# A top-k attention kernel with a gated feed-forward block: where the sine, the gate and the argument reduction stand in the first twelve units

## The chip, the cores and the metric

The kernel runs on one core of one Trainium2 chip. Its time is the device time in microseconds (us) of one execution; lower is better. A core has five engines with a queue of instructions each: TensorE (PE, with its weight loads PEld), VectorE (DVE), ScalarE (ACT), GpSimd (POOL) and SyncE (SP), which here only issues DMAs. Each queue is worked off in order, and engines wait for one another by semaphores.

## What is computed

The reference takes q, k and v of 8 batches, 8 heads, 576 positions and a head size of 64, and keeps in each row of scores the 32 largest:

```python
scores = scale * np.matmul(q, k.transpose(0, 1, 3, 2))
kth = np.partition(scores, -top_k, axis=-1)[..., -top_k:-top_k + 1]
scores = np.where(scores >= kth, scores, -1000000000.0)
scores = scores - np.max(scores, axis=-1, keepdims=True)
attn = np.exp(scores)
attn = attn / (np.sum(attn, axis=-1, keepdims=True) + 1e-09)
...
h = x @ w_in
g = h * np.cos(h)
return (g @ w_out).astype(np.float32)
```

Here x is the attention's output with the heads side by side: 4608 rows of 512. The weights w_in (512 x 2048) and w_out (2048 x 512) arrive as 64-bit numbers and are turned into 32-bit ones on the chip.

## The kernel before

The work is cut into 144 units. A unit is 128 rows of queries of one pair of heads; four units with the same rows make a block, whose feed-forward part can start when all four are done. The loop at the end runs over the units, and its body `slot(i, u, w, x, z)` is one slot of a software pipeline written out by hand: VectorE searches the top 32 of unit u = i, ScalarE masks and exponentiates unit w = i - 1, GpSimd splits unit x = i - 2 into 16-bit halves (L424, L426) which SyncE writes out and reads back transposed (L434, L440), and in even slots TensorE multiplies units z = i - 4 and i - 3 with v (`values`, L477). Scores of coming units (`scores`, L226) are computed in even slots, mostly for two units at once; `take_scores` (L236, L237) copies them out of PSUM on ScalarE.

Between these stand steps of the feed-forward part, handed to TensorE by `feed(n)` as a credit allows: `ff1` (L537, xT by w_in into mm) and `ff2` (L612, g by w_out into o). For each 1024 columns of a block there is a chain: `take_first` copies mm/(2 pi) into g (L551) and a rounded value into x (L553) on ScalarE; the argument is reduced on GpSimd in two steps, `reduce_first` (L573) and `reduce_second` (L582); `sines` computes the cosine as a sine on ScalarE (L592, another table than the exponential's); `gate` multiplies g by it on GpSimd (L599). A block has two such chains. `feed` lets `ff2` begin some feeds after the gate was recorded (`can_second`), and only for weights that were added in an earlier slot.

The dictionary `ff` carries a flag `late`. When it is set, `take_first` marks its result with the slot's number and `reduce_first` leaves a result of the same slot for the next one. Before the change it is off in a slot's first half and on in the second.

In the first slots the weights are decoded as well: `load_weights` at a slot's start (L120, on SyncE's queue in slots 0 and 1, then on ScalarE's), `decode_first` on ScalarE (L133, L136) near its end, and in the following slot `decode_second` on VectorE (a shift, L144) and `decode_third` on GpSimd (an integer add, L154). The last add, of w_out15, stands in slot 12.

In units 7 to 11 (`BUSY`) VectorE makes both folds of the scores (L247, L255); in the others that fold, GpSimd makes the lower one (L265, L274).

Of the kernel before, what the change touches and what calls it, by code (L numbers as in the profile page):

```python
# [30 lines left out]
def kernel(  # L31
# [16 lines left out]
    NP = H // 2  # L48
# [47 lines left out]
    ff = {"live": 0, "tick": 0, "now": 0, "credit": 0.0, "end": False, "kind": 0, "half": 0, "open": 0, "late": False}  # L96
# [6 lines left out]
    def load_weights(n, queue):  # L103
        for _ in range(n):
            i = wq["next"]
            if i >= len(chunks):
                return
            src, dst = chunks[i]
            if not DECODE:
                queue.dma_start(out=dst, in_=src)  # L110
                wq["next"] = wq["done"] = i + 1
                continue
            spare = i < 3 * XB and i % 2 == 1 and staged(1) < XB
            if spare:
                st = ffw.tile([P, CW, 2], I32, tag="x", name="st", bufs=XB)
            elif staged() + ff["live"] >= CHUNKS:
                return
            else:
                st = ffw.tile([P, CW, 2], I32, tag="g", name="st", bufs=CHUNKS)
            queue.dma_start(out=st.rearrange("p w i -> p (w i)"), in_=src)  # L120
            wq["loaded"].append((st, dst, int(spare)))
            wq["next"] = i + 1
# [16 lines left out]
    def decode_second(n):  # L139

        for _ in range(min(n, len(wq["second"]))):
            st, w, spare = wq["second"].popleft()
            wi = w.bitcast(I32)
            nc.vector.tensor_scalar(  # L144
                out=wi, in0=wi, scalar1=3, scalar2=None, op0=ALU.logical_shift_left
            )
            wq["third"].append((st, w, spare))
# [144 lines left out]
    def topk_first(u, w):  # L292

        u["top"] = tops[u["n"] % len(tops)]
        merges = w and w["folds"]
        if merges:
            merge_first(w)
        if u["folds"]:
            if u["n"] not in BUSY:
                fold_sum(u)  # L300
            fold_high(u)
        else:
            u["rest"] = work.tile([P, 2, S], F32, tag="rest", name="rest", bufs=1)
        if merges:
            merge_second(w)
        if u["folds"] and u["n"] in BUSY:
            fold_now(u)
        topk_round(u, 0, [lambda: bounds(w), lambda: distances(w)] if w else ())

    def topk_round(u, rnd, between=(), ahead=None):  # L310
        top, rest, lasts = u["top"], u["rest"], TOPK // 8 - 1
        end = TOPK - 1 - 8 * rnd
        at = top[:, :, end : end - 8 if rnd < lasts else None : -1, 0]
        if u["folds"]:
            search(
                at, rest[:, :, HS:S] if rnd == 0 else rest[:, :, 0:HS], rest[:, :, 0:HS], rnd < lasts,
                between if rnd < lasts else (),
            )
        else:
            search(at, u["s"] if rnd == 0 else rest, rest, rnd < lasts, between)  # L320
        if rnd < lasts:
            return
        del u["rest"]
        if u["folds"]:
            low = u.pop("low")
            for k in range(TOPK // 16):
                more = k < TOPK // 16 - 1
                if ahead and not more:
                    take_values(ahead)
                search(  # L330
                    top[:, :, 1 + 8 * k : 9 + 8 * k, 1], low, low, more,
                    () if more or rnd < lasts else between,
                )
# [16 lines left out]
    def search(to, src, rest, more, between=()):  # L350
        for j in range(2):
            nc.vector.max(to[:, j], src[:, j])  # L352
            if between:
                between[j]()
        if more:
            for j in range(2):
                nc.vector.match_replace(rest[:, j], to[:, j], src[:, j], NEG)  # L357
# [61 lines left out]
    def split(u):  # L419


        s = u.pop("s").rearrange("p j k -> p (j k)").bitcast(U16)
        halves = work.tile([P, 2, 2 * S + P], U16, tag="halves", name="halves", bufs=1)
        nc.gpsimd.tensor_copy(out=halves[:, :, 0 : 2 * S], in_=s.rearrange("p (k h) -> p h k", h=2))  # L424
        rden = u.pop("rden").bitcast(U16).rearrange("p (j h) -> p h j", h=2)
        nc.gpsimd.tensor_copy(  # L426
            out=halves[:, :, 2 * S :].rearrange("p h (j d) -> p h j d", j=2),
            in_=rden.unsqueeze(3).to_broadcast([P, 2, 2, D]),
        )
        u["halves"] = halves  # L430

    def write_halves(u):
        rows = u["rows"] = dram.tile([P, 2, 2 * S + P], U16, tag="rows", name="rows")
        nc.sync.dma_start(out=rows, in_=u.pop("halves"))  # L434

    def transposes(u):
        rows = u.pop("rows").rearrange("q h k -> (q h) k")
        pT = u["pT"] = work.tile([P, 2 * NT + 2, P], F32, tag="pT", name="pT", bufs=3)
        words = pT.rearrange("p c q -> p (c q)").bitcast(U16)
        nc.sync.dma_start_transpose(  # L440
            out=words.rearrange("p (c q) -> p c q", c=2 * NT + 2), in_=rows
        )
# [36 lines left out]
    def take_values(us):  # L479
        blk, hp, n = block_of[us[0]["tok"]], us[0]["hp"], len(us)  # L480
        if "xT" not in blk:
            blk["xT"] = work.tile([P, NP, P], F32, tag="xT", name="xT", bufs=5)
        for i, u in enumerate(us):
            to, o, pT = blk["xT"][:, hp + i], room[0][:, i * P : (i + 1) * P], u.pop("pT")
            if u["paired"]:
                nc.vector.tensor_tensor(out=to, in0=o, in1=pT[:, 2 * NT + 1], op=ALU.mult)
            else:
                nc.scalar.copy(out=to, in_=o)
        blk["left"] -= n
        blk["tick"] = ff["tick"]  # L490
# [94 lines left out]
    def sines(least):  # L585

        n = sum(c[3] < ff["now"] for c in waiting)
        if n == 0 or (n < least and waiting[0][3] + 2 > ff["now"]):
            return
        for _ in range(n):  # L590
            blk, g, x, _ = waiting.popleft()
            nc.scalar.activation(out=x, in_=x, func=AF.Sin, bias=halfpi, scale=TWO_PI_BELOW)  # L592
            sined.append((blk, g, x))

    def gate(n):
        for _ in range(min(n, len(sined))):
            blk, g, x = sined.popleft()
            eng = nc.vector if ff["end"] else nc.gpsimd
            eng.tensor_tensor(out=g, in0=g, in1=x, op=ALU.mult)  # L599
            blk["gated"].append(ff["tick"])  # L600
# [87 lines left out]
    for n in range(NP, len(order)):  # L688
        i = last[order[n - 5]] if n >= 5 else 0
        load_at(max(i, 2 * NP + 2), load_qk, *order[n])  # L690
        i = last_values[order[n - 6]] if n >= 6 else 0
# [13 lines left out]
    def send(x):  # L705

        split(x)
        write_halves(x)
        transposes(x)

    def slot(i, u, w, x, z):
        n = (3, 4, 3, 2)[i] if i < NP else 2 if i < 2 * NP else 3
        if i < NP:
            for load, b, hp in at_once[i]:
                load(b, hp)
        load_weights(n, nc.sync if i < 2 else nc.scalar)
        if x:
            send(x)
        ff["late"] = False
        topk_first(u, w)  # L720
        fold_low(u)
        topk_round(u, 1)
        topk_round(u, 2)
        decode_second(NP)
        decode_third()
        reduce_first()
        reduce_second()
        made = scored.get(i, [])
        if z:
            take_banks()  # L730
        feed(1)

        for m in made:
            scores(m)
        if z:
            values(z)


        late = len(made) > 0

        decoding = i < 3 * NP
        if i % 2 or decoding:
            sines(1)
        if w:
            mask(w)
        take_banks()
        if w and late:
            exponentials(w)
        take_scores(units[i + 1])
        if w and not late:  # L750
            exponentials(w)
        topk_round(u, 3, both(w), z)
        ff["late"] = True
        if i in at_slot:
            load, b, hp = at_slot[i]
            load(b, hp)
        gate(1)
        feed(1 if len(made) == 2 else 2)
        take_banks()
        decode_first(NP)  # L760
        reduce_first()
        reduce_second()
        feed(1 if len(made) == 2 else 3)
        if i == LAST:
            sines(1)
# [110 lines left out]
```

## Time and profile before

| what | value |
|---|---|
| median of 8 runs | 1468.9 us (1467.34 to 1471.08) |
| the profiled execution | 1469.89 us |
| its span, first to last instruction | 1468.1 us |
| mean granted clock of TensorE | 0.985 |
| busy: PE, PEld | 1390.7 us (95%), 998.2 us (68%) |
| busy: DVE, ACT, POOL | 1362.2 us (93%), 1087.9 us (74%), 1156.7 us (79%) |
| largest shares of the chain that ended last | PE 84%, DVE 8%, ACT 4%, DMA 2% |
| one shift of weights on VectorE (L144) | 0.419 us median |
| one table load on ScalarE | 1.28 us |

A line of the timeline gives the start and the length in us, the engine, the line of the kernel, the operation, the tile written and those read, how many instructions are merged, and in brackets how long the engine sat idle before and for whom. A line of waits gives the engine and line that waited, for whom, the total in us, how often, and the longest. A line of a table by stretch gives the stretch, its length, the busy time and instructions of PE, PEld, DVE, ACT and POOL, then TensorE's granted clock, the busy share of the DMA engines and GB/s. One matmul of 32-bit numbers leaves two records in the trace, so a step of `ff2` (two matmuls) is four records of L612, and a step of `ff1` (eight matmuls) sixteen of L537.

### The profile page before, as it was taken

To read this page: it belongs to the slowest core of one execution; us is meant where nothing else is said; L and a number is where in the kernel's file an instruction comes from. 1 tells how busy PE (TensorE), PEld (TensorE's weight loads), DVE (VectorE), ACT (ScalarE), POOL (GpSimd) and SP (SyncE) were. 2 spreads that over 40 slices of the span, in tenths; PEclk is the share of its full clock that TensorE was granted. 3 is DMA by queue.
4 is the path that set the end of the run, shared out by engine and by line. 5 is a ranking of instruction groups with operands and counts; after the bars stand their busy time and mean duration, and the time that the engine had idled before them with its cause. 6 is when DMAs were issued, how large, how long until landed. Compare 5 with 4: busy or idle time off the path is not lost.

```text
span 1468.1 us, 30229 instructions
## 1 busy us (share of the span) xinstructions
PE 1390.7 (95%) x10288; PEld 998.2 (68%) x10288; DVE 1362.2 (93%) x5213; ACT 1087.9 (74%) x1910; POOL 1156.7 (79%) x812
## 2 busy tenths in 40 slices
PE   4367999999999999999999999999999999999998
PEld 2254767777777767777777767777777777777765
DVE  7997999999999999999999999999999999999831
ACT  5786777777777777777777777777777777777651
POOL 5856888888888887888888888888888888888410
PEclk9788999999999999999999999999999999999999
DMA  8986586656665566657655666657665565655200
GB/s 259 276 232 172 161 196 176 159 162 174 189 159 151 153 185 180 167 145 192 181 167 146 149 179 181 173 151 183 188 168 146 151 171 168 162 151 151 62 8 15
DMA packets 427434, 240.00 MB, mean 163 GB/s; under 512 B 375952, under 2 KB 392592, under 8 KB 427280
## 3 DMA queue, kind: packets, MB, share of 16 engines
q1 hardware_dynamic: 418704, 216.88, 56.1%
q10 hardware_dynamic: 8576, 21.19, 4.2%
q8 instruction: 81, 1.33, 0.4%
q14 instruction: 73, 0.60, 0.1%
HBM read 45.09 MB, written 101.19 MB: 100 GB/s over the span
## 4 chain that ended last, share of the span: by engine, by line
PE 84%; DVE 8%; ACT 4%; DMA 2%; SPq 0%; issue 0%; POOL 0%; ACTq 0%; POOLq 0%
PE o L612 32%; PE mm L537 32%; PE rim L477 10%; PE sc L226 8%; DVE top L352 3%; DVE rest L357 2%; PE rim L226 2%; DMA v<-in_v_dram 1%; ACT s L391 1%; DMA st<-in_moe_w_in_dram 1%; DVE rest L247 1%; ACT s L383 1%; DMA pT<-rows 0%; ACT L391 0%; DVE low L357 0%
## 5 line engine op out<-in xcount | busy, mean ns | idle before, releaser
L537 PEld LDWEIGHTS mm<-xT,w_in 128*128 128x128 f32 x4608 | 539.4, 193 | 70.0 <-issue 64.3
L612 PE MATMUL o<-w_out,g 128*128 128x512 f32 x1152 | 539.1, 602 | 22.7 <-POOL g L599 19.4
L537 PE MATMUL mm<-xT,w_in 128*128 128x128 f32 x4608 | 542.4, 276 | 3.2 <-ACT x L553 2.5
L352 DVE MAX8 top<-rest 128x8 f32<-128x288 f32 x1148 | 481.0, 454 | 0.0
L424 POOL COPY halves<-s 128x2304 uint16<-128x2304 uint16 x140 | 294.5, 2104 | 150.3 <-ACT s L391 149.7
L357 DVE MATCH_REPLACE8 rest<-top,rest 128x288 f32<-128x288 f32 (+1 forms) x860 | 377.2, 446 | 0.0
L612 PEld LDWEIGHTS o<-w_out,g 128*128 128x128 f32 x1152 | 203.4, 191 | 211.7 <-issue 187.4
L352 DVE MAX8 top<-low 128x8 f32<-128x288 f32 x568 | 240.3, 449 | 0.0
L391 ACT ACTIVATE s<-s,nd 128x576 f32<-128x576 f32 x288 | 220.2, 767 | 0.8
L383 ACT ACTIVATE s<-s,top 128x576 f32<-128x576 f32 x288 | 206.1, 765 | 0.0
L274 POOL TENSOR_TENSOR low<-low,rest 128x576 int32<-128x576 int32 x137 | 193.4, 1412 | 10.7
L265 POOL TENSOR_TENSOR low<-s 128x576 int32<-128x576 int32 x137 | 193.2, 1410 | 6.3 <-ACT s L237 5.1
L226 PE MATMUL sc<-k,q 64*128 64x448 f32 (+1 forms) x640 | 158.8, 590 | 34.2 <-DVE rest L247 13.5
L551 ACT ACTIVATE g<-mm 128x512 f32<-128x512 f32 x144 | 85.8, 596 | 129.6 <-PE mm L537 125.5
L582 POOL TENSOR_TENSOR x<-g,x 128x1024 f32<-128x1024 f32 x68 | 160.8, 2365 | 5.7
L477 PE MATMUL rim<-pT,v 128*64 128x128 f32 (+1 forms) x2560 | 158.7, 268 | 3.3 <-DMA pT<-rows 3.3
L599 POOL TENSOR_TENSOR g<-g,x 128x1024 f32<-128x1024 f32 x68 | 160.7, 2363 | 1.3 <-ACT x L592 1.3
L477 PEld LDWEIGHTS rim<-pT,v 128*64 128x64 f32 x2560 | 132.0, 138 | 13.8 <-issue 5.0
L236 ACT COPY s<-sc 128x896 f32<-128x896 f32 x144 | 129.2, 897 | 12.0 <-PE sc L226 11.6
L237 ACT COPY s<-rim 128x256 f32<-128x256 f32 x144 | 55.0, 382 | 94.5 <-PE rim L477 94.5
L357 DVE MATCH_REPLACE8 low<-top,low 128x288 f32<-128x288 f32 x284 | 123.8, 444 | 0.0
L226 PEld LDWEIGHTS sc<-k,q 64*128 64x128 f32 (+1 forms) x640 | 47.3, 182 | 98.3 <-DVE rest L357 47.9
(59 smaller groups left out, 1333.5 us busy)
## 6 DMA issues: line engine op xcount, KB each, us to landing
rows<-halves SPq DMA_DIRECT2D x140, 640.0 KB, 3.0
out_dram<-ob ACTq DMA_DIRECT2D x36, 256.0 KB, 2.2
q<-in_q_dram SPq DMA_DIRECT2D x31, 288.0 KB, 3.7
v<-in_v_dram SPq DMA_DIRECT2D x32, 256.0 KB, 3.5
st<-in_moe_w_out_dram ACTq DMA_DIRECT2D x16, 512.0 KB, 5.0
st<-in_moe_w_in_dram SPq DMA_DIRECT2D x10, 512.0 KB, 6.7
k<-in_k_dram SPq DMA_DIRECT2D x31, 144.0 KB, 3.6
k<-in_k_dram SPq DMA_DIRECT2D x32, 128.0 KB, 3.7
```

Source lines behind the costliest of these rows:

```text
L226: nc.tensor.matmul(to[r0 : r0 + rows, j, 0 : k1 - k0], st["q"][d, q0 : q0 + rows], st["k"][d, k0:k1], start=True, stop=True,)
L265: nc.gpsimd.tensor_tensor(out=u["low"].bitcast(I32), in0=s[:, :, 0:HS], in1=s[:, :, HS:S], op=ALU.add)
L274: nc.gpsimd.tensor_tensor(out=low, in0=low, in1=u["rest"][:, :, HS:S].bitcast(I32), op=ALU.subtract)
L352: nc.vector.max(to[:, j], src[:, j])
L357: nc.vector.match_replace(rest[:, j], to[:, j], src[:, j], NEG)
L383: nc.scalar.activation(out=s[:, j], in_=s[:, j], func=AF.Prelu, bias=less[:, j, 1:2], scale=1.0, alpha=FAR)
L391: nc.scalar.activation(out=s[:, j], in_=s[:, j], func=AF.Exp, bias=nd[:, j : j + 1], scale=SCALE, accum_out=den[:, j, 0:1],)
L424: nc.gpsimd.tensor_copy(out=halves[:, :, 0 : 2 * S], in_=s.rearrange("p (k h) -> p h k", h=2))
L477: nc.tensor.matmul(o[d, to], lhsT, rhs, start=c == 0, stop=c == NT)
L537: nc.tensor.matmul(mm[:, at : at + w], w_in[f // FC][:, c, (f % FC) * P : (f % FC + 1) * P], blk["xT"][:, c], start=c == 0, stop=c == NC - 1,)
L582: nc.gpsimd.tensor_tensor(out=x, in0=g, in1=x, op=ALU.subtract)
L612: nc.tensor.matmul(o, g[:, at : at + P], w_out[f], start=f == 0, stop=f == NF - 1)
```

## The change

`decoding` is true in slots 0 to 11 and is now set at the slot's start. In these slots `sines(1)` and `gate(1)` are called after the third round of the search and so ahead of the weights' shifts and adds; the split of `send(x)` already stands before them. The call of `sines` in the middle of the slot is left to odd slots from 12 on. The gate of the slot's second half (L757 before) stays for all slots; in a decoding slot it finds something only if the first call left it. The flag `late` stays off in the second half of a decoding slot, so that a result of `take_first` is reduced at the end of the same slot.

```diff
         if x:
             send(x)
+        decoding = i < 3 * NP
         ff["late"] = False
         topk_first(u, w)
         fold_low(u)
         topk_round(u, 1)
         topk_round(u, 2)
+        if decoding:
+            sines(1)
+            gate(1)
         decode_second(NP)
         decode_third()
         reduce_first()
@@
-        decoding = i < 3 * NP
-        if i % 2 or decoding:
+        if i % 2 and not decoding:
             sines(1)
         if w:
             mask(w)
@@
         topk_round(u, 3, both(w), z)
-        ff["late"] = True
+        ff["late"] = not decoding
```

By the two programs' instruction order, VectorE's queue is unchanged, and PE's differs only from the last `ff1` step of the first block to that of the second. On GpSimd the first reduction moves from behind slot 8's adds to before slot 8's split, the first gate from slot 9 to slot 8 (behind the split, ahead of the adds of w_out6 and w_out5), and the second gate ahead of slot 10's adds instead of behind them. On ScalarE the first sine moves from slot 9's middle to slot 8's start, and the second stays the first activation of slot 10; in slot 12 the copies of mm (L551, L553) come before the sine instead of after the mask.

## The prediction

> **What bounds the kernel now.** I read the busy tenths of the page first, then stages, then who waited, then the queues around the longest wait. I call a slot by the number i of its unit; on VectorE the slots begin at 79.8 (slot 7), 90.1, 100.8, 111.6 (slot 10), 134.1, 144.7, 154.5 and 165.2 us (slot 14), read from the group of L340, which opens a slot. The busy time by slot:
>
> ```profile
> 100.80:111.60 10.80, 0.00 (x0) 0.00 (x0) 10.69 (x40) 10.74 (x19) 8.10 (x7) 0.60 0.56 187
> 111.60:134.10 22.50, 15.90 (x85) 8.92 (x86) 12.90 (x43) 11.12 (x19) 15.77 (x10) 0.74 0.63 176
> 134.10:144.70 10.60, 9.39 (x62) 7.29 (x60) 10.60 (x40) 9.51 (x19) 3.40 (x4) 1.00 0.79 187
> ...
> 165.20:1350.00 1184.80, 1184.56 (x8985) 852.76 (x8984) 1161.99 (x4528) 919.61 (x1602) 1013.99 (x693) 1.00 0.63 167
> ```
>
> After the length come PE, PEld, DVE, ACT, POOL, then clock and DMA. From slot 14 to 1350 us PE is idle 0.24 us in 1184.8, DVE 2%. So TensorE's work bounds the kernel from slot 14 on, and what a change there cannot shorten it can only start earlier. Before that, slot 9 has no matmul at all and slot 10 lasts 22.5 us where its neighbours last 10.6 to 10.8. The waits between 98 and 132 us, total, times, longest:
>
> ```profile
> PE o L612 <- POOL g L599: 19.4, 1, 19.4
> ...
> ACT s L236 <- PE sc L226: 7.6, 1, 7.6
> ```
>
> PE stands 19.4 us before the first output matmul, which needs the gated product g. PE is in order: slot 10's scores stand behind, ScalarE's copy of them waits 7.6 us, and VectorE 9.6 us for that copy:
>
> ```profile
> 96.56 2.05 PE L537 MATMUL mm<-xT,w_in 128*128 128x128 f32 x16
> 118.04 9.78 PE L612 MATMUL o<-w_out,g 128*128 128x512 f32 x16 [19.43 <-POOL g L599]
> 127.75 1.02 PE L226 MATMUL sc<-k,q 64*128 64x448 f32 x4
> ...
> 132.75 0.49 DVE L486 TENSOR_TENSOR xT<-rim,pT 128x128 f32<-128x128 f32 x2 [9.60 <-ACT s L237]
> ```
>
> GpSimd's queue shows why g is late: slot 8's adds (97.42), then the reduction (L573, L582), slot 9's split and adds, a second reduction, and only then the gate (115.62):
>
> ```profile
> 97.42 2.53 POOL L154 TENSOR_TENSOR w_out<-w_out,st 128x512 int32<-128x512 int32 x2 [5.35 <-ACT s L237]
> 99.92 1.05 POOL L573 TENSOR_SCALAR x<-x 128x1024 f32<-128x1024 int32 x1
> 101.06 2.38 POOL L582 TENSOR_TENSOR x<-g,x 128x1024 f32<-128x1024 f32 x1
> ...
> 108.44 3.78 POOL L154 TENSOR_TENSOR w_out<-w_out,st 128x512 int32<-128x512 int32 x3 [2.62 <-ACT s L237]
> ...
> 115.62 2.36 POOL L599 TENSOR_TENSOR g<-g,x 128x1024 f32<-128x1024 f32 x1
> ```
>
> **What the Trainium skill says.** "SBUF — State Buffer", section "SBUF: two separate sides": VectorE and GpSimd share a port pair as an exclusive lock for a whole instruction. The trace agrees: VectorE's shift (L144, median 419 ns) took 2260 ns once, at 118.06, over GpSimd's split at 117.93. "TensorE: Matmul & The Clock Gate", section "What's actually happening": an idle window of about 3.4 us halves the clock and a busy one restores it. The trace agrees: the granted clock is 0.5 between 104 and 116 us, and the o matmuls begin at 118.04 with 0.855 us a record, later 0.43. "ScalarE: Activation LUTs", section "What ACT_TABLE_LOAD costs": 1283 ns plus a drain of about 1380 ns. The trace agrees on 1.28 us only: the sine starts at 104.48, 1.30 after its load at 103.18.
>
> **The change part by part.** No instruction is added or dropped: by the instruction order both have 138 table loads, and VectorE's order is equal. Only two sines, two gates and one reduction move, around slots 7 to 12; from o's first matmul of the second block on (164.93 us before), PE's order is the same. So the effect is how much earlier PE gets there.
>
> Slot 7's end. With the late flag off, the first reduction goes from behind slot 8's adds to before slot 8's split. Its input (ACT L553) ends at 88.6, GpSimd is free at 89.6: 1.1 + 2.3 us, ready at 93.05 instead of 103.4. The split moves from 89.62 to 93.05 and ends at 95.45 (2.05 + 0.36). Its write on SP moves from 93.33 to 95.5, the transpose behind it from 96.84 to about 99, landing 6.5 us later at 105.5; its reader is slot 10's values: nothing, if these come after 105.5.
>
> Slot 8's sine, now ahead of the mask and exponentials. ScalarE ends its decode at 90.75, loads the table (1.28), waits until 93.05, sine 1.05 (start to start), the two L551/L553 1.05, mask 1.45, table 1.28, exponentials 1.54, copies 1.1: the copy of rim ends at about 100.6 instead of 97.05. VectorE wanted it at 99.49: a cost of about 1.1.
>
> Slot 8's gate, behind the split: 95.45 to 97.8, instead of 115.62 to 117.98. Behind it on GpSimd stand two adds, for which ACTq's next two weight loads wait (98.74, 99.98: about 1.1 later, hidden by ScalarE's three decodes, 3.4 us). VectorE's shifts want to start at 96.53 and may be locked out until 97.8: 0 to 1.3; this runs beside the 1.1, so slot 8 costs VectorE 1.1 to 1.3 together; I take 1.3. Slot 10 then begins at 112.9.
>
> PE. Four o matmuls (8 records, 3.44) run from 97.9 to 101.3, eight mm (1.8) to 103.1, three more o to 105.7. The eighth needs w_out7, added last in slot 9: VectorE's shifts 107.22 + 1.3, ready at 109.6, three adds (3.78): 113.4. PE idles 7.7 us and is at half clock: scores from about 115.1 instead of 127.75, values done by 120 to 122 instead of 132.3.
>
> Slot 10. The second reduction ends at 113.4 + 3.45 = 116.9 (needed by the sine); sine 118, mask 119.4, table 120.7, exponentials 122.3, copies 123.4. VectorE needs that copy at 122.4, or at 124.7 if its shifts (119.4) are locked out by the gate that GpSimd starts just then (2.3). So VectorE passes L486 at 123.4 to 124.7 instead of 132.75: 8.1 to 9.3 earlier. Where the stall goes: what is late next is this sine chain, by about 1 us.
>
> Slots 11 to 13 run at VectorE's pace (10.6, 9.8, 10.7) in both. In slot 12 GpSimd's add, reduction, split, fold and gate follow without a gap (151.16 to 163.4), shifted by the same 8.1 to 9.3: the gate for the second block ends at 154.1 to 155.3, and PE has nothing else left. Before, PE came there at 164.93, since mm took 5.47 instead of 3.57 at half clock: 9.6 to 10.8 earlier. PE's wait there, about 3 us, may bring half clock again; the price of a window is 1.7 to 1.9, from that mm. From here PE is bound by its own work. Gain 7.7 to 10.8; Slot 14's scores and values follow VectorE, so its 8.1 to 9.3 is the likelier part of that span, and I take its middle, 8.7.
>
> Against the profiled execution (1469.89 us, span 1468.1) this gives 1461.2 and a span of 1459.4; the median of eight is 1468.9, 1.0 lower, so **1460.2 us**.
>
> **The rivals.**
> A, forecast: the stall becomes a short one; gain 6 to 11.5.
> B: both lockouts (1.3 + 2.3), half clock through slot 10's scores and values (up to 4.6 us more, the length that they take at full clock from 127.75 on) and one window more at slot 14 (1.9) add up beyond what I took: gain 3 to 6, middle 1464.4. For it: PE is idle 7.7 us in slot 9, with a cold array. Against: VectorE needs slot 10's copy only when ScalarE's chain is done.
> C: the gain is used up before saturation, because slot 12's GpSimd chain does not follow VectorE but the weights, whose loads share DMA engines that are 56 to 91% busy here: the gate stays near 163.4, 1468.9. Against: the last weight's add ended at 152.4 only since VectorE's shift was at 150.48.
> D, slower: the earlier start changes the phase of the engines in the saturated loop, VectorE's folds wait on split or gate at another place, and PE idles where it had 0.24 us. There are about 63 pairs of slots (1184.8 by 18.8); 0.14 us in each cancels 8.7, above 0.18 the kernel is slower by over 0.2%. At 0.25: +7, 1475.9. Against: VectorE has 2% (0.36 us a pair) to give before PE feels it.
> That the change does nothing is excluded by the order of instructions.
>
> **How the numbers follow.** A 0.70, B 0.13, C 0.08, D 0.09. Two runs of this kernel can be told apart from about 0.2%, 2.9 us. Faster is A and B, 0.83; same 0.08; slower 0.09. The range 1457.0 to 1466.0 is a gain of 11.9 to 2.9: it takes in the upper end of A and all of B, and leaves out C and D. A's own range is 1457.4 to 1462.9.
>
> **What would show it.** The wait of o for g falls from 19.4 to about 1 us at 97 us, and a wait of about 8 us for w_out (L154) appears at 113; scores of slot 10 near 115; VectorE's 9.6 us shrinks to 0 to 1.5; slot 14 begins near 156; from there the same 18.7 us a pair. Wrong would be: a copy of slot 8 that ends past 102, slot 10's scores after 120, or PE idle over 5 us between slot 14 and 1340 us.

## The result, and the profile after

| | before | after |
|---|---|---|
| median, runs side by side | 1469.81 us (1466.84 to 1477.11, 32 runs) | 1460.61 us (1458.12 to 1462.9, 11 runs) |
| the profiled execution, its span | 1469.89, 1468.1 us | 1462.54, 1460.8 us |
| start of slot 7 to start of slot 14 | 85.37 us | 77.21 us |
| start of slot 7 to the end | 1388.28 us | 1378.52 us |
| mean granted clock of TensorE | 0.985 | 0.974 |

The ratio is 0.9935 with a 95% interval of 0.9923 to 0.9946: 9.2 us less between the medians, against 1460.2 us and a gain of 8.7 predicted.

One thing has to be set aside first. The two programs are the same up to slot 7, yet in the profiled run of after slot 7 starts at 82.28 us, 2.46 us later than before's 79.82: loads of k landed late (PE waited for them 15.2 us in the first 160 us, before 5.7), and slot 4 lasted 12.67 us instead of 10.27. That is this one execution's, not the change's: e7 and e8 below, the same program up to slot 8, come there at 79.15 and 78.91. After's lower mean clock is of the same kind, since its half clock lies mostly ahead of slot 7 (the mean up to 82.28 us is 0.63). So I compare from the start of slot 7 on, where the profiles differ by 1388.28 - 1378.52 = 9.76 us, while the spans differ by 7.3. "On the scale of before" below means less 2.46 us.

The busy time by slot in the profile of after, slots 8, 9, 10, 11 and 13 and then the stretch from slot 14 on; the columns are those of before:

```profile
92.58:104.61 12.03, 8.63 (x73) 5.78 (x73) 11.95 (x42) 11.03 (x19) 11.25 (x8) 1.00 0.93 172
104.61:115.23 10.62, 5.15 (x24) 2.93 (x22) 10.62 (x40) 9.58 (x19) 4.30 (x5) 0.87 0.84 256
115.23:128.17 12.94, 12.05 (x74) 7.39 (x75) 12.94 (x42) 9.91 (x16) 12.49 (x9) 0.71 0.67 230
128.17:138.80 10.63, 8.33 (x61) 6.84 (x60) 10.63 (x40) 8.89 (x18) 4.48 (x5) 1.00 0.83 218
...
148.67:159.49 10.82, 7.39 (x41) 5.09 (x40) 9.20 (x36) 10.29 (x17) 9.39 (x7) 1.00 0.65 186
159.49:1340.00 1180.51, 1179.09 (x8975) 851.40 (x8975) 1159.31 (x4519) 916.17 (x1598) 1011.64 (x693) 1.00 0.63 168
```

Slot 10 is 12.94 us long instead of 22.43, and VectorE is busy in all of it. Slot 8 has become longer, 12.03 instead of 10.69. Slot 9 had no matmul, now it has 24 records. From slot 14 on PE is idle 1.42 us in 1180.51, of which 1.26 are one new wait at its start (167.91 below). What PE waited for between 100 and 134 us:

```profile
PE o L612 <- POOL w_out L154: 6.3, 1, 6.3
PE rim L477 <- DMA pT<-rows: 3.4, 1, 3.4
```

The 19.4 us for the gated product are gone; in their place stand 6.3 us for a weight and 3.4 us for a transpose's DMA. PE's timeline shows where:

```profile
100.46 1.09 PE L477 MATMUL rim<-pT,v 128*64 128x128 f32 x16 [3.40 <-DMA pT<-rows]
101.70 3.70 PE L612 MATMUL o<-w_out,g 128*128 128x512 f32 x8
...
107.02 2.74 PE L612 MATMUL o<-w_out,g 128*128 128x512 f32 x6
...
116.08 2.08 PE L612 MATMUL o<-w_out,g 128*128 128x512 f32 x2 [6.32 <-POOL w_out L154]
118.09 1.87 PE L226 MATMUL sc<-k,q 64*128 64x448 f32 x4
...
157.66 1.98 PE L612 MATMUL o<-w_out,g 128*128 128x512 f32 x4 [2.16 <-POOL g L599]
...
166.03 0.61 PE L537 MATMUL mm<-xT,w_in 128*128 128x128 f32 x4
167.91 3.39 PE L537 MATMUL mm<-xT,w_in 128*128 128x128 f32 x28 [1.26 <-DVE xT L486]
```

The first output matmul starts at 101.70 (before 118.04), slot 10's scores at 118.09 (before 127.75), and the second block's first at 157.66 (before 164.93). Counted from the start of slot 7 the last is 75.38 instead of 85.11, 9.73 us earlier. PE does not keep all of that. In slot 14, four records into a step of `ff1`, it waits 1.26 us for VectorE (L486); before ran the same 32 records without a wait:

```profile
173.20 3.81 PE L537 MATMUL mm<-xT,w_in 128*128 128x128 f32 x32
```

From the fifth record on (167.91; before 173.64) PE is 8.19 us earlier, which is what VectorE is: its slot 14 begins 85.37 - 77.21 = 8.16 us earlier. The other 1.6 of the 9.76 us come later; more on them under "What the gain is". GpSimd's queue:

```profile
95.55 2.10 POOL L424 COPY halves<-s 128x2304 uint16<-128x2304 uint16 x1
97.95 2.35 POOL L599 TENSOR_TENSOR g<-g,x 128x1024 f32<-128x1024 f32 x1
101.00 2.54 POOL L154 TENSOR_TENSOR w_out<-w_out,st 128x512 int32<-128x512 int32 x2 [0.70 <-DVE w_out L144]
...
121.83 2.54 POOL L599 TENSOR_TENSOR g<-g,x 128x1024 f32<-128x1024 f32 x1
124.73 2.55 POOL L154 TENSOR_TENSOR w_out<-w_out,st 128x512 int32<-128x512 int32 x2 [0.36 <-DVE w_out L144]
```

And VectorE beside it, the shifts of slots 8 and 10 and the step (L486) that needs ScalarE's copy:

```profile
98.99 1.92 DVE L144 TENSOR_SCALAR w_out<-w_out 128x512 int32<-128x512 int32 x2
103.29 0.49 DVE L486 TENSOR_TENSOR xT<-rim,pT 128x128 f32<-128x128 f32 x2
121.64 3.00 DVE L144 TENSOR_SCALAR w_out<-w_out 128x512 int32<-128x512 int32 x2
126.87 0.47 DVE L486 TENSOR_TENSOR xT<-rim,pT 128x128 f32<-128x128 f32 x2
```

The gate of 97.95 runs to 100.30 and the pair of shifts, begun at 98.99, lasts 1.92 us; the gate of 121.83 runs to 124.37 and the pair lasts 3.00. A free pair takes 0.75 (seen below). VectorE waits nowhere here for ScalarE's copy: its 9.60 us are gone.

### The profile page after: what moved, and what is told of

It is laid out like the page before. It is cut to its first block, busy times and chain, and to the rows that moved or that the text cites. A ratio compares the mean times of both kernels' runs of the same rounds, so it can differ in the third digit from the quotient of the medians.

```text
span 1460.8 us, 30230 instructions
## 1 busy us (share of the span) xinstructions
PE 1385.9 (95%) x10288; PEld 998.6 (68%) x10288; DVE 1364.2 (93%) x5213; ACT 1087.7 (74%) x1910; POOL 1156.6 (79%) x812
## 4 chain that ended last, share of the span: by engine, by line
PE 84%; DVE 8%; ACT 4%; DMA 2%; SPq 1%; issue 0%; POOL 0%; ACTq 0%; POOLq 0%
PE mm L537 32%; PE o L612 31%; PE rim L477 10%; PE sc L226 8%; DVE top L352 4%; DVE rest L357 2%; PE rim L226 2%; DMA rows<-halves 1%; ACT s L391 1%; ACT s L383 1%; DVE rest L247 1%; ACT L391 1%; DMA st<-in_moe_w_in_dram 1%; DVE low L357 0%; DMA pT<-rows 0%
## 5 line engine op out<-in xcount | busy, mean ns | idle before, releaser
L551 ACT ACTIVATE g<-mm 128x512 f32<-128x512 f32 x144 | 85.7, 595 | 128.5 <-PE mm L537 124.4
```

## Experiments

My theory: the gain is the first chain's (reduction, sine and gate before slot 10's scores), it ends when VectorE and the next late weight set slot 10's end, and what it is worth is how much earlier VectorE, and PE with it, gets to slot 14, since PE is the bound from there. The rivals: the second chain matters too; the gate's place, behind the split and ahead of the adds, matters; PE's work before slot 14 is itself a bound; the new wait for w_out7 holds the gain back. A further question is what makes slot 8 longer.

All times are medians; the ratios are to the kernel before, run on the same chip. The slot lengths are of each kernel's profile, on VectorE, in us.

| kernel | median | ratio, 95% interval | slot 8 | 9 | 10 | 7 to 14 | 15 to end |
|---|---|---|---|---|---|---|---|
| before | 1469.81 | | 10.69 | 10.84 | 22.43 | 85.37 | 1293.5 |
| after | 1460.61 | 0.9935 (0.9923 to 0.9946) | 12.03 | 10.62 | 12.94 | 77.21 | 1291.9 |
| e1, flag only | 1464.67 | 0.9965 (0.995 to 0.998) | 11.08 | 11.90 | 14.18 | 79.50 | 1291.6 |
| e2, order only | 1461.52 | 0.9944 (0.9926 to 0.9963) | 10.68 | 12.45 | 13.40 | 78.15 | 1293.2 |
| e3, slot 8 only | 1458.95 | 0.9935 (0.9912 to 0.9957) | 12.04 | 10.62 | 12.21 | 76.31 | 1290.7 |
| e4, slot 10 only | 1469.73 | 0.999 (0.9977 to 1.0003) | 18.21 | 14.79 | 18.20 | 92.82 | 1292.7 |
| e5, gate behind the adds | 1466.64 | 0.9976 (0.9965 to 0.9987) | 12.04 | 12.04 | 10.93 | 81.65 | 1291.5 |
| e10, first gate behind the adds | 1459.61 | 0.9925 (0.9904 to 0.9945) | 12.05 | 12.35 | 10.92 | 76.79 | 1291.9 |
| e6, copies first | 1462.62 | 0.995 (0.993 to 0.997) | 11.90 | 10.63 | 12.92 | 77.06 | 1292.7 |
| e11, slot 8 only, copies first | 1461.71 | 0.9948 (0.9927 to 0.9969) | 12.34 | 10.62 | 12.21 | 76.62 | 1291.9 |
| e7, work in slot 9 | 1459.26 | 0.9936 (0.9914 to 0.9958) | 12.03 | 10.63 | 12.94 | 77.21 | 1292.0 |
| e8, work in slot 20 | 1464.68 | 0.9975 (0.9962 to 0.9987) | 12.04 | 10.62 | 12.93 | 77.19 | 1297.1 |
| e9, w_out7 first | 1460.24 | 0.9939 (0.9919 to 0.9958) | 13.78 | 10.63 | 12.83 | 78.86 | 1291.3 |
| e12, four moves | 1460.45 | 0.993 (0.9909 to 0.9951) | 11.60 | 10.62 | 12.22 | 76.27 | 1292.7 |

The column "7 to 14" says how early VectorE gets to slot 14. In every one of these profiles PE's first matmul there that reads VectorE's result of L486 (before at 173.64 us) follows it within 0.2 us: it comes 8.19 us earlier than before's in after (VectorE 8.16), 7.07 in e2 (7.22), 3.76 in e5 (3.72), 9.14 in e12 (9.10).

### Half the change: the flag, or the order

e1 is before with the flag alone, e2 is after without it.

```diff
e1, against before:
-        ff["late"] = True
+        ff["late"] = i >= 3 * NP
e2, against after:
-        ff["late"] = not decoding
+        ff["late"] = True
```

> Of the change only the flag: late stays off in the second half of slots 0 to 11, so the first reduction comes at the end of slot 7 and its sine falls into slot 8's middle by itself; the calls of sines and gate stand where they stood before. Theory (what counts is one threshold: the first gate must end before w_out7 is added, since o's eighth matmul waits for that weight anyway): the gate ends near 102 to 104 us, well ahead of w_out7 near 113, and the whole gain is there, 8 to 10.5 us, ratio about 0.9935, with VectorE's slot 8 not locked out. Rival (each part brings its share, the flag 3.45 us of reduction): gain 3 to 5 us.

> Of the change only the order: sines and gate behind the search's third round, ahead of the adds; the flag as before, so that the reduction stays behind slot 8's adds. The gate then stands behind slot 9's split, ending near 108 us, before slot 9's adds. Theory (threshold at w_out7): again the whole gain, 8 to 10.5 us. Rival (shares add up): 4 to 6 us, and this one and the flag alone sum to the 9 us of both.

The flag alone gains 0.35%, the order alone 0.56%, the two together 0.65%. The intervals are too wide to tell 0.65 from the sum, 0.91, but the profiles do: up to slot 14 the flag wins 5.9 us, the order 7.2 and both 8.2, so the halves are no shares of a sum. In e2 the first product comes at 109.56, after a wait about half as long as before's:

```profile
109.56 9.83 PE L612 MATMUL o<-w_out,g 128*128 128x512 f32 x16 [10.36 <-POOL g L599]
```

and that alone takes slot 10 from 22.43 to 13.40 us, near after's 12.94. VectorE's wait for ScalarE's copy there, 9.60 us before, is down to 2.62:

```profile
124.32 0.49 DVE L486 TENSOR_TENSOR xT<-rim,pT 128x128 f32<-128x128 f32 x2 [2.62 <-ACT s L237]
```

So most of PE's 10.36 us is hidden. In e1 the wait is 2.33 us, yet its runs gain about 5 us and not the 8 to 10.5 that I expected. Its profile:

```profile
101.73 7.97 PE L612 MATMUL o<-w_out,g 128*128 128x512 f32 x14 [2.33 <-POOL g L599]
112.30 1.75 PE L612 MATMUL o<-w_out,g 128*128 128x512 f32 x2 [2.60 <-POOL w_out L154]
...
122.66 1.79 PE L477 MATMUL rim<-pT,v 128*64 128x128 f32 x16 [4.21 <-DMA pT<-rows]
```

Slot 10's values wait 4.21 us for a transpose, and slots 8 to 10 sum to 37.16 us where after has 35.59. That is only 1.6 us more, and the profiled execution, 1461.48 us, is among the faster ones of 15 runs that lie between 1460.1 and 1471.75, so it does not show what the others lose; what spreads them so, when after's lie within 4.8 us, stays open.

### One chain alone

e3 applies the change to the first chain only (slot 8), e4 to the second only (slot 10).

```diff
e3, against after (e4: 10 for 8, 9 for 7):
-        if decoding:
+        if i == 8:
             sines(1)
             gate(1)
@@
-        if i % 2 and not decoding:
+        if i != 8 and (i % 2 or decoding):
             sines(1)
@@
-        ff["late"] = not decoding
+        ff["late"] = i != 7
```

> The counterpart of slots 9 and 10 alone: the new flag in slot 7 and the new places in slot 8, so only the first chain moves. Theory (the first gate is all that PE's long wait hung on): the whole gain of the change, 7 to 10 us faster than before. Rival (the second gate ahead of slot 10's adds brings a share, since with both gates behind adds 5 us of the gain were gone): 3 us or more of the gain missing.

> The new places for slots 9 and 10 alone, that is for the second chain; the first chain as before. Theory: the 19.4 us wait for the first gate stays, and the time with it: within 1.5 us of before. Rival (the second gate ahead of slot 10's adds is what lets PE go on): 3 us or more faster.

e3 has the whole gain, e4 none that can be told from nothing. In e3 PE comes to slot 9's last weight and finds the same kind of wait as in after:

```profile
98.43 3.70 PE L612 MATMUL o<-w_out,g 128*128 128x512 f32 x8
...
114.03 2.08 PE L612 MATMUL o<-w_out,g 128*128 128x512 f32 x2 [7.53 <-POOL w_out L154]
```

In e4 the long wait for the product is still there:

```profile
103.81 1.98 PE L477 MATMUL rim<-pT,v 128*64 128x128 f32 x16 [9.46 <-DMA pT<-rows]
125.25 9.47 PE L612 MATMUL o<-w_out,g 128*128 128x512 f32 x16 [15.46 <-POOL g L599]
```

(Its profiled execution is its longest, 1476.17 us: a transpose landed late in slot 8, PE waited 9.46 us and slot 8 lasted 18.21. So e4's median counts here, not its slot lengths.) The rival that the second chain matters falls: e3's interval would leave it up to 3 us, but in e3's profile VectorE gets to slot 14 0.9 us earlier than in after's.

### The gate's place

e5 puts both gates behind the adds; e10 only the first, with the rest as in e3.

```diff
e5, against after (e10: with i == 8 for decoding, and e3's other lines):
         if decoding:
             sines(1)
-            gate(1)
         decode_second(NP)
         decode_third()
+        if decoding:
+            gate(1)
```

> The changed kernel with the early gate moved behind the weights' adds, the sine where the change has it. Theory: the first gate ends about 2.5 us later, still ahead of w_out7; VectorE's shifts meet no gate on the shared port (1.3 us in slot 8 and 2.3 us in slot 10 are not paid), but the second gate comes 2.5 us later and PE waits for it in slot 10: between 1 us faster and 3 us slower than the changed kernel, 6 to 10 us faster than before. Rival (the place ahead of the adds is what the gain rests on): at least 4 us of it gone.

> As the run with slots 7 and 8 alone, but the first gate stands behind slot 8's adds; the second gate is recorded and issued where the kernel before has it. Both gates behind the adds cost 5 us of the gain; this tells whose place that was. Theory (the second: it was recorded early, so that PE was handed o's ninth matmul early, and issued late, so that PE waited 6.9 us for it): with the second gate back in its old place the gain is whole, 7 to 10 us. Rival (the first gate's place ahead of the adds): 4 us or more of it gone, as before.

e5 loses over half of the gain; by itself that suggests that the first gate has to stand ahead of the adds. e10 refutes it: with the first gate behind the adds the gain is whole, 0.9925. e10 leaves the whole second chain where before has it, so it clears the first gate; that the second gate is what costs in e5 is read from PE's waits there:

```profile
103.23 5.70 PE L612 MATMUL o<-w_out,g 128*128 128x512 f32 x8 [5.58 <-POOL g L599]
...
127.33 3.78 PE L612 MATMUL o<-w_out,g 128*128 128x512 f32 x4 [6.86 <-POOL g L599]
```

and GpSimd in e5, in slot 10:

```profile
122.41 2.53 POOL L154 TENSOR_TENSOR w_out<-w_out,st 128x512 int32<-128x512 int32 x2 [2.06 <-issue]
124.91 2.38 POOL L599 TENSOR_TENSOR g<-g,x 128x1024 f32<-128x1024 f32 x1
```

The gate is recorded in slot 10, so `can_second` lets the second chain's output matmuls into PE's queue in that slot; but on GpSimd it stands behind two adds that start when VectorE's shifts are done (121.52 to 122.27), and runs at 124.91 to 127.29. PE waits 6.86 us with slot 11's work behind it, and slots 11 and 12 become 13.21 and 12.12 us (after: 10.63 and 9.87). The first wait, 5.58 us, is longer than after's but harmless: e10 has the same place for that gate and waits 5.01.

### Is PE's work before slot 14 a bound?

e7 adds 20 matmuls into a bank that no step reads then, in slot 9, and e8 the same in slot 20; what the kernel computes is unchanged.

```diff
e7, against after (e8: i == 20):
         reduce_second()
+        if i == 9:
+            for _ in range(20):
+                nc.tensor.matmul(room[1][:, 0:P], w_in[0][:, 0, 0:P], ident, start=True, stop=True)
         made = scored.get(i, [])
```

> The changed kernel with 20 matmuls more in slot 9 (identity, 128 by 128, into PSUM that nobody reads; the output is unchanged), about 4.5 us at full clock, where PE waits 6.3 us for w_out7 and loses its clock. Theory (PE's time before slot 14 is not what bounds): within 1.5 us of the changed kernel; faster rather than slower, since the array stays warm into slot 10. Rival (every matmul counts): 4.5 us slower than the changed kernel.

> The same 20 matmuls in slot 20 of the changed kernel, where PE never idles. Theory (PE's own work bounds from slot 14 on, so what it does later is lost to the end): 4 to 5 us slower than the changed kernel, at 1464.5 to 1466. Rival (VectorE, busy 98%, is the real bound and PE only looks full): 0 to 1.5 us slower.

In slot 9 they cost nothing: slots 8 to 10 and the stretch from 15 on are those of after within 0.2 us. They run from 100.79 to 105.49, and PE's wait for w_out7 shrinks from 6.32 us to 3.10. In slot 20 the stretch from 15 on grows from 1291.9 to 1297.1 us, and the median is 5.4 us above e7's. The same stretch of e8, from 1.1 us ahead of slot 14's start:

```profile
155.00:1340.00 1185.00, 1184.94 (x9007) 854.68 (x9006) 1158.02 (x4515) 915.94 (x1598) 1010.54 (x691) 1.00 0.63 167
```

PE is idle 0.06 us in 1185.00. So in the stretch from slot 14 on PE's work counts in full, about 5.1 / 20 = 0.26 us for each matmul (the added ones themselves run for 4.6 us, from 215.7 to 220.3), and in slot 9 not at all; no other slot before 14 was tried. This is why an earlier start of that stretch is an earlier end.

### The new wait for w_out7

e9 takes the oldest weight first, so that w_out7 is the first of slot 9's three adds and not the last.

```diff
e9, against after:
-            st, w, _ = wq["third"].pop()
+            st, w, _ = wq["third"].popleft()
```

> The changed kernel with each slot's adds in the other order, so that w_out7 is added first in slot 9: PE's eighth o matmul starts 2.5 us earlier and slot 10's scores with it. Theory (in slot 10 the sine's chain on ScalarE, behind all three adds, and VectorE's lockout by the gate set the pace, not w_out7): at most 1.5 us faster than the changed kernel. Rival (the new wait for w_out7 has taken the place of the old one): 2 to 2.5 us faster.

The time is after's, 0.9939. In e9's profile the wait for w_out7 is 1.67 us, and slot 10 takes 12.83 us instead of 12.94: the 6.3 us at 116.08 cost nothing, since VectorE, busy in all of slot 10, sets its end. (Slot 8 is 13.78 us long in this profile, in which PE waited 5.11 us there for a transpose.)

### What lengthens slot 8

In slot 8 of after two things are late for VectorE: the shifts (locked behind the gate) and ScalarE's copy of rim (behind the sine). e10 above takes the first away. e6 takes the second away in slots 8 and 10 by putting the copies ahead of the exponentials; e11 does so in e3's slot 8.

```diff
e6, against after (e11: i != 8, with e3's lines):
-        late = len(made) > 0
+        late = len(made) > 0 and i not in (8, 10)
```

> The changed kernel with ScalarE's copies of the scores ahead of the exponentials in slots 8 and 10, the two slots that now hold two table loads. The copies then wait neither for the second table load (1.28 us) nor the exponentials (1.54 us). Theory (VectorE's cost in slot 8, 12.03 instead of 10.3 to 10.7 us, is the gate on the shared port, with the late copy only beside it): slot 8 stays above 11.6 us, and the time within 1 us of the changed kernel. Rival (the late copy is the cost): slot 8 back to 10.7 us and 1 to 2 us faster.

> The run with slots 7 and 8 alone, with ScalarE's copies ahead of the exponentials in slot 8. A try for a faster version: the second chain stays as before, so that no gate is issued ahead of slot 10's shifts. Theory (what slot 8 pays is the shared port): within 1 us of the run with slots 7 and 8 alone. Rival (the late copy): 1 to 1.3 us faster, 1457.5 or less.

VectorE in e10, no gate beside the shifts:

```profile
96.18 0.75 DVE L144 TENSOR_SCALAR w_out<-w_out 128x512 int32<-128x512 int32 x2
...
100.50 0.49 DVE L486 TENSOR_TENSOR xT<-rim,pT 128x128 f32<-128x128 f32 x2 [1.28 <-ACT s L237]
```

and in e6, no late copy:

```profile
97.95 1.95 DVE L144 TENSOR_SCALAR w_out<-w_out 128x512 int32<-128x512 int32 x2
...
102.13 0.47 DVE L486 TENSOR_TENSOR xT<-rim,pT 128x128 f32<-128x128 f32 x2
```

In e10 the shifts take 0.75 us and VectorE then waits 1.28 us for the copy; in e6 it waits for nothing, and the shifts take 1.95. Slot 8 is 12.05 and 11.90 us: each cause alone costs about as much as both, since they lie side by side, and to remove one gains nothing. No run removes both. Against my expectation, e6 and e11 are not within 1 us of the kernels that they change: their medians lie 2.0 us above after's and 2.8 above e3's. The intervals overlap, and up to slot 14 the profiles differ by 0.3 us at most, so a loss isn't shown either.

### A version with all of these at once

e12 has e9's order of the adds and e6's copies, puts the reduction and the adds of a decoding slot behind the middle `take_banks`, and the loads of weights of slot 6 and later behind the sine.

```diff
e12, against after, beside e6's and e9's lines:
-        load_weights(n, nc.sync if i < 2 else nc.scalar)
+        if i < 6:
+            load_weights(n, nc.sync if i < 2 else nc.scalar)
...
             sines(1)
+            if i >= 6:
+                load_weights(n, nc.scalar)
             gate(1)
+        if not decoding:
+            load_weights(n, nc.scalar)
         decode_second(NP)
-        decode_third()
-        reduce_first()
-        reduce_second()
+        if not decoding:
+            decode_third()
+            reduce_first()
+            reduce_second()
...
         take_banks()
+        if decoding:
+            reduce_first()
+            reduce_second()
+            decode_third()
```

> A try for a faster version, four moves together on the changed kernel: w_out7 added first; the slot's reduction ahead of the adds where its input is there; ScalarE's weight loads behind the sine instead of ahead of it (in slot 10 the table load waited 1.9 us behind them); the copies ahead of the exponentials in slots 8 and 10. Theory (slot 10's 12.94 us is the sine's chain and the lockout by the gate, both gone when the reduction runs in slot 9): slot 10 down to 10.7 to 11 us and the time 1.5 to 3 us below the changed kernel. Rival (PE's own work from slot 14 on hides what VectorE wins): no more than 0.5 us.

Slots 8 and 10 became 0.43 and 0.72 us shorter; slot 10 was to lose about 2. The lockout that the moves were to remove stayed: the pairs of shifts took 1.67 us in slot 8 and 1.75 in slot 10. And the time is after's, 0.993: the 1.5 to 3 us that I expected did not come. The stretch from slot 15 on took 1292.7 us, 0.8 more than after's, which takes most of the 0.94 us between slots 7 and 14 back in the profiles; a difference of this size can't be told from none here. No version is measurably faster than after.

## Why the prediction was right

Each time is on the scale of before.

- **Slot 7's end and slot 8.** Gate predicted at 95.45, measured 95.49; end of the copy of rim 100.6, measured 100.8; cost to VectorE 1.3, measured 12.03 - 10.69 = 1.34. That the late copy and the lockout lie beside each other and do not add is what e6 and e10 show.
- **PE.** The output matmul that needs w_out7 was predicted at 113.4, measured 113.62; slot 10's scores at 115.1, measured 115.63. One term was missing: PE waited 3.40 us for the transpose of slot 8's values (before 0.72), so the wait for g is 0 and not about 1, and that for w_out7 6.3 and not 7.7. In e7 the transpose costs 1.55 us and the wait for g is 0.44. The term is hidden, since what PE does next waits for w_out7 anyway.
- **Slot 10.** VectorE passes L486 at 124.41; predicted 123.4 to 124.7, the upper end with the lockout, which came: 3.00 us for a pair of shifts against 0.75. The stall left 8.34 us earlier than before's 132.75.
- **Slots 11 to 13** run at 10.63, 9.87 and 10.82 us (before 10.62, 9.85, 10.65), as said, and slot 14 starts 8.16 us earlier.
- **The second block's start.** PE was predicted there 9.6 to 10.8 us earlier, measured 9.73; the wait for g there about 3 us, measured 2.16. The window at half clock behind that wait, for which I set off up to 1.9 us, did not come: in after's profile the granted clock is 0.5 from 112.4 to 122.6 us and 1.0 from there to 1365 us, and the window that before has at 160.9 to 164.3 is gone. Whether it comes was chance, and it made no difference: in e8, the same program up to there, the clock was 0.5 from 155.4 to 158.8, and in slot 14 PE was 8.0 us earlier than before, in after 8.2.
- **What the gain is.** Within 7.7 to 10.8 I took 8.7, the middle of VectorE's 8.1 to 9.3, because slot 14 follows VectorE. That held: VectorE comes 8.16 us earlier and holds PE, which came earlier still, back to 8.19. The profiles gain 9.76 from slot 7 on, and for the other 1.6 the prediction has no term. In before's profile the stretch from slot 15 on, 1293.5 us, is the longest of all but e8's, and even e4, which gains nothing, is 0.8 us shorter there; so part of the 1.6 is likely before's own execution, and the rest stays open. The medians, 9.2 us apart, don't decide it: their interval, 7.9 to 11.3 us, holds 8.2, 8.7 and 9.8 alike. That 1460.2 and 1460.61 lie as close as 0.4 us is more than this noise lets one claim.
- **From slot 14 on** PE is idle 1.42 us in 1180.51, 1.26 of them for VectorE in slot 14, within the 5 that I allowed. e8 shows that its work is the bound there.
- **Rivals.** B needed half clock in slot 10 to pass to VectorE: the clock is 0.5 to 122.6, and both lockouts occurred, but slots 11 to 13 together lost 0.2 us. C (slot 12's gate tied to the weights) fails: that gate came with VectorE. D (a new phase in the saturated part) fails: the stretch from 15 on is 1291.9 us, before 1293.5. e5 shows that there was a way to lose over half of the gain that I had not listed: a gate that is recorded early and issued late.

## What to carry to other kernels

When one engine is bound from some point on, price a change in the start-up by when that engine can run on from there without a wait: PE got to the second block 9.7 us earlier, but VectorE held it back to 8.2. Work that it does earlier may be free: 20 more matmuls in slot 9 cost nothing, in slot 20 they cost about 5 us. Halves of a reordering need not add up, because a wait only has to fall below the next one: check each half, and don't read one reversal as the cause (e5 blamed the wrong gate until e10). A step whose bookkeeping releases another queue's work should be issued where it is recorded, or the other engine stands waiting with everything behind it.

## What the runs showed of the hardware

- The Trainium skill, "SBUF — State Buffer", section "SBUF: two separate sides", has VectorE and GpSimd share a pair of ports as an exclusive lock that one instruction holds to its end. The runs agree: one shift of integers on VectorE, 422 ns in the median, took 2578 ns beside a GpSimd multiplication of 2.54 us, and 0.75 us a pair when no gate lay beside it (e10).
- Waits for DMAs vary from one execution to the next more than I had reckoned with: after, e7 and e8 are the same program up to slot 8, and slot 7 starts at 82.28, 79.15 and 78.91 us in their profiles, and PE waits 3.40, 1.55 and 2.20 us for the transpose in slot 8. The longest wait for a transpose was 9.46 us (e4), where before had 0.72 in that place.
- The Trainium skill, "TensorE: Matmul & The Clock Gate", section "What's actually happening", has a window of about 3.4 us in which the array is idle halve the clock. In these profiles the changes of the granted clock lie multiples of 3.41 us apart (after: half clock from 112.37 to 122.61, three of them), but a window lost the clock without being idle throughout. PE's wait for g before the second block is 2.12 to 2.16 us in e2, e6, e7, e8 and after. In e2, e6 and e8 it lies within one window, and the next window ran at half clock (e8: 155.38 to 158.79). In after and e7 the edge of a window divides it (after: 1.25 us before 156.75, 0.92 behind), and the clock stayed 1.0.
- Worked out in the same way from the records of PE, for every window between 80 and 235 us that had full clock, in all 14 profiles: with up to 1.81 us without a matmul (e12) the next one kept full clock, with 1.95 us (e8) or more it did not. One window falls outside this (e9, 1.67 us, half clock after it).
